# Recurrent-memory attention with a routed MLP: which queue loads the left sums, and where the routed rows are read back

## The chip, the cores and the metric

The kernel runs on one core of a Trainium2 chip. The metric is the device time of one execution in microseconds; lower is better. Engines are TensorE (PE, with its weight loads as PEld), VectorE (DVE), ScalarE (ACT), GpSimd (POOL) and SyncE (SP). SyncE, ScalarE and GpSimd can issue transfers (DMAs); SyncE's and ScalarE's go out on hardware queues, GpSimd's on a software queue, and all of them run on the core's 16 DMA engines.

## The reference

For one sequence of 2048 tokens of width 1024 the output is the sum of the input, an attention with a memory that is handed from segment to segment, and an MLP that only two tokens take.

```
x  = A_x                                   # 2048 x 1024
xn = layernorm(x)
# attention: 64 segments of 32 tokens, 32 heads of 128
for s in range(64):
    h = concat([mem, xn[32 s : 32 s + 32]])          # 8 + 32 rows
    q, k, v = h Wq, h Wk, h Wv
    o = softmax(mask(q k^T / sqrt(128))) v Wo
    mem = o[:8];  A[32 s : 32 s + 32] = o[8:]
# MLP on the two tokens with the largest r = xn @ w_r
y = (silu(xs @ w_gate) * (xs @ w_up)) @ w_down       # 1024 -> 3584 -> 1024
B = xn;  B[idx] += sigmoid(r[idx]) * y
out = x + A + B
```

## The kernel before, in words

The memory makes the 64 segments a chain: a segment can begin only when the first rows of the segment before are finished. Of each segment only 24 token rows and the 8 memory rows go through the chain. The last 8 token rows of every segment (the "left" rows, 512 in all) feed nothing later. Their queries, keys and values are made once ahead of the chain; within the chain only their attention sums are made (tile OTL), and GpSimd stores them to DRAM (`ol_d`, four tensors of 16 segments each; `store_sums`, line 639). Their projection with Wo is left for the tail.

Weights of the attention are 64 granules of 512 KB. Most stay resident on the chip; the streamed ones are fetched again in every segment by SyncE, five slots ahead (`fetch`, line 401). The end of a segment is a loop over the 16 granules of Wo (`for w in range(16)`): granule w of Wo is used and, if streamed, the next fetch goes out. In the last segment, at w == 2, the space of eight resident granules (area big0) has become free. It turns into OTA, which will hold all 512 left rows' sums, 16 pieces of 256 KB (k = 0 to 15, `load_left_out`, line 629), four for each block of 128 left rows.

The order of all instructions is written out by hand; nothing is reordered. A transfer of SyncE or ScalarE, and one of GpSimd likewise, takes one of eight completion counters in turn, and waits for the transfer that had it before. So at most eight of a queue are under way.

The tail, after the last segment's Wo loop:

- SyncE's queue holds, in this order: 16 tiles of w_gate (448 KB each, issued from line 451 as homes come free during the last segment), the left sums k 4 to 7, the four blocks of x rows (XLS, line 893), six tiles of w_up, the left sums k 8 to 15, four tiles of w_up into the first half of OTA, six more w_up and 16 transfers of w_down (line 460).
- `left_sums` (line 898): VectorE takes mean and variance of the four XLS blocks and turns each into x plus its normed value.
- `left_rows_out(0)`, half A (line 919): TensorE multiplies blocks 0 and 1 of OTA with all of Wo, 64 matmuls a block into two PSUM accumulators each (tags kept0 to kept3, one buffer each). VectorE adds the accumulators to XLS (line 931), GpSimd stores the block (line 932).
- The two routed token rows are copied into a zero-padded tile RX (32 columns for each of 8 chunks, lines 949 to 951). The first 20 pieces of gate and up follow (`gate_up(0, early)`, line 959); each piece frees a home, into which SyncE fetches the next tile.
- An activation of one column asks for the Silu table (line 969). Then half B, `left_rows_out(1)`: blocks 2 and 3, into the same four accumulators.
- GpSimd reads the two routed rows of the output back from DRAM into ROW (line 973). Their place is only known at run time, so the read-back stands behind every store of the output. The other 12 pieces of up follow, Silu of gate on ScalarE (line 982), the product (line 985), transposes, and w_down (line 1001, YP, 112 matmuls).
- VectorE adds YP times the gate value to ROW (line 1004); SyncE stores the first row, ScalarE the second (line 1006). The program then closes with a drain of each engine and a barrier (line 1037).

Of the kernel before, what the change touches and what calls it, by code (L numbers as in the profile page):

```python
# [12 lines left out]
ACTF = mybir.ActivationFunctionType  # L13
# [17 lines left out]
def kernel(  # L31
# [16 lines left out]
    nc = tc.nc  # L48
    P = 128
    Bsz, S, D = A_x.shape  # L50
# [8 lines left out]
    KC = D // P  # L59
# [70 lines left out]
    def room(g, name):  # L130
        if g not in place:
            return home(g, [P, 2048], BF16, name)[:, :]
        tag, i = place[g]
        return areas[tag][:, i, :]
# [23 lines left out]
    I8 = CT[0:1, 24:32].bitcast(U32)  # L158
# [34 lines left out]
    for s in range(4):  # L193
        nc.vector.tensor_copy(out=SELM[:, s, 0:XM, :],
                              in_=IDENT[:, 32 * s:32 * s + XM].unsqueeze(2).to_broadcast([P, XM, 4]))
# [104 lines left out]
    RXT = const.tile([P, 2 * KC], BF16, name="RXT").rearrange("p (k c) -> p k c", c=2)  # L300
    SIG = const.tile([P, 1], F32, name="SIG")
    routed_rows = []
# [134 lines left out]
    moe = [("gu", w, kc, fh) for w in range(2) for kc in range(KC) for fh in range(2)]  # L437
# [191 lines left out]
    def load_left_out(k, queue):  # L629
        queue.dma_start(out=areas["big0"][:, 4 * k:4 * k + 4, :], in_=ol_d[k // 4][:, 4 * (k % 4):4 * (k % 4) + 4, :])  # L630
# [39 lines left out]
    for s in range(NSEG):  # L670
# [178 lines left out]
        for w in range(16):  # L849
            if w == 5:  # L850
                attend(1, 0)
            if w == 8:
                attend(1, 1)
            if w == 2 and s + 1 == NSEG:
                OTA = area("big0", [P, NSEG, XL * H], "OTA")
                for k in range(4):
                    load_left_out(k, nc.gpsimd)
            Gv = granule(48 + w)
            if s + 1 == NSEG and 48 + w in streamed:
                left_in_slots[48 + w] = Gv  # L860
            project(WO, w, Gv, lhs_main, w == 15)
            if w == 9 and s + 1 < NSEG:
                load_qkl(s + 1)
                bring_back(FIRST_KEPT, 1, "bE", nc.scalar.copy)
                bring_back(FIRST_KEPT, 2, "kt", nc.vector.tensor_copy)
            if w == 11 and s + 1 == NSEG:
                store_sums()
            if w == 10 and s + 1 < NSEG:
                nxt["st"] = new_st(s + 1)
            after(s, 48 + w)  # L870
# [9 lines left out]
            ST = nxt["st"]  # L880


    for k in range(4, 8):
        load_left_out(k, nc.sync)
    WOS = {g: res_tiles.get(g, left_in_slots.get(g)) for g in sorted(range(48, 64), key=lambda g: g in streamed)}
    XLS = [room(resident[k], "XLS") for k in range(2)]
    T2 = one.tile([P, 512], BF16, tag="bC", name="T2")
# [10 lines left out]
    def left_sums():  # L898
        ml = T2[:, 100:108].rearrange("p (t c) -> p t c", c=2)
        sl = T2[:, 108:124].bitcast(F32).rearrange("p (t c) -> p t c", c=2)  # L900
        for t in range(4):
            row_stats(left_x(t), T2[:, 128:152].bitcast(F32).rearrange("p (c s) -> p c s", c=2), ml[:, t, :])
        sd_rows(ml, T2[:, 124:128])
        nc.vector.tensor_copy(out=sl[:, :, 0], in_=ml[:, :, 0])
        nc.vector.reciprocal(out=sl[:, :, 1], in_=ml[:, :, 1])
        for t in range(4):
            m, r = sl[:, t, 0:1], sl[:, t, 1:2]
            nc.vector.tensor_scalar(out=m, in0=m, scalar1=r, scalar2=-1.0, op0=ALU.mult, op1=ALU.mult)
            nc.vector.tensor_scalar(out=r, in0=r, scalar1=1.0, scalar2=None, op0=ALU.add)
            nc.vector.tensor_scalar(out=left_x(t), in0=left_x(t), scalar1=r, scalar2=m, op0=ALU.mult, op1=ALU.add)  # L910
# [8 lines left out]
    def left_rows_out(k):  # L919
        WD = [[psK.tile([P, 512], F32, name=f"WD{2 * b + c}", tag=f"kept{2 * b + c}") for c in range(2)] for b in range(2)]  # L920
        for b in range(2):
            for i, (g, Gv) in enumerate(WOS.items()):
                for hs in range(2):
                    for c in range(2):
                        nc.tensor.matmul(WD[b][c][:, :], lhsT=OTR[:, P * (2 * k + b):P * (2 * k + b + 1), 2 * (g - 48) + hs],
                                         rhs=Gv[:, D * hs + 512 * c:D * hs + 512 * (c + 1)],
                                         start=(i + hs == 0), stop=(i == 15 and hs == 1))
            x = left_x(2 * k + b)
            for c in range(2):
                xc = x[:, 512 * c:512 * (c + 1)]  # L930
                nc.vector.tensor_tensor(out=xc, in0=xc, in1=WD[b][c][:, :], op=ALU.add)
            nc.gpsimd.dma_start(  # L932
                out=out2.rearrange("(t s r) d -> t s r d", t=4, s=16)[2 * k + b, :, XM:SEG, :], in_=x)

    T0 = room(resident[2], "T0")
    left_sums()
    left_rows_out(0)
    T3 = one.tile([P, 256], BF16, tag="bA", name="T3")
    ROW = T3[:, 0:256]

    def quarters(c):
        return T3[c:c + 97:32, 0:256]

    def routed_out(v):
        return out2[bass.ds(v, 1), :].rearrange("o (g d) -> (o g) d", g=4)

    ends = (nc.sync, nc.scalar)
    GU = [[psA.tile([P, 512], F32, tag="acc", name=f"GA{fh}") for fh in range(2)], [BS, BT]]
    RX = T2[:, 256:512].rearrange("p (k r) -> p k r", r=32)
    nc.vector.memset(T2[:, 256:512], 0.0)  # L950
    nc.vector.tensor_copy(out=RX[:, :, 0:2], in_=RXT)

    pieces = [(w, kc, fh) for w in range(2) for kc in range(KC) for fh in range(2)]

    def gate_up(i0, i1):
        for w, kc, fh in pieces[i0:i1]:
            Gt = moe_tiles["gu", w, kc, fh]
            for g in range(4):
                nc.tensor.matmul(GU[w][fh][32 * g:32 * g + 32, 0:FQ], lhsT=RX[:, kc, :], rhs=Gt[:, FQ * g:FQ * (g + 1)],
                                 start=(kc == 0), stop=(kc == KC - 1), tile_position=(0, 32 * g), skip_group_check=True)  # L960
            free_homes.append(moe_home["gu", w, kc, fh])
            fetch_moe()
# [3 lines left out]
    fetch_moe()  # L966
    early = len(moe)
    gate_up(0, early)
    nc.scalar.activation(out=T2[:, 126:127], in_=T2[:, 124:125], func=ACTF.Silu)
    left_rows_out(1)  # L970
    nc.vector.memset(ROW, 0.0)
    for c in range(2):
        nc.gpsimd.dma_start(out=quarters(c), in_=routed_out(routed_rows[c]))
    gate_up(early, len(pieces))
    assert not moe
    end_rows = [ends[c].value_load(I8[0:1, c:c + 1], min_val=0, max_val=S - 1) for c in range(2)]
    HR = T0[:, 0:2 * FQ]
    SG = [[T0[:, 1024 + 448 * i:1024 + 448 * (i + 1)].bitcast(F32) for i in range(2)],
          [one.tile([P, 224], F32, tag=tag, name="SG") for tag in ("kt", "bE")]]
    for fh in range(2):  # L980
        for i in range(2):
            nc.scalar.activation(out=SG[fh][i], in_=GU[0][fh][:, 224 * i:224 * (i + 1)], func=ACTF.Silu)
    for fh in range(2):
        for i in range(2):
            nc.vector.tensor_tensor(out=HR[:, FQ * fh + 224 * i:FQ * fh + 224 * (i + 1)], in0=SG[fh][i],
                                    in1=GU[1][fh][:, 224 * i:224 * (i + 1)], op=ALU.mult)
# [55 lines left out]
```

## Time and profile before

| | |
|---|---|
| median of 3 runs | 1846.6 us (1841.18 to 1846.63) |
| the profiled execution's own time | 1831.82 us |
| its span, first to last instruction | 1830.1 us |
| mean granted TensorE clock | 0.987 |
| busy: PE, PEld, DVE, ACT, POOL | 1551.3, 830.0, 880.2, 779.7, 325.0 us |
| HBM read, written | 652.90 MB, 29.89 MB (373 GB/s over the span) |
| SyncE's queue, GpSimd's queue | 624.84 MB, 47.59 MB |

Rows of the profile give a start in microseconds from the start of the span, the time, the engine, the line of the kernel, the operation and its tiles (output, arrow, inputs), then how many. In square brackets stands the idle time of the engine ahead of the instruction and what ended it. "SPq" and "ACTq" are the sequencers that issue transfers. A row on transfers gives the size of one and the median time from issue to landing. The matmul records of a few instructions can be missing.

### The profile page before, as it was taken

The numbers are of one execution on the slowest core, as the hardware profiler recorded it, in microseconds if no ns is written. First come the engines' busy times: TensorE is split into PE (matmuls) and PEld (weight loads), VectorE is DVE, ScalarE is ACT, GpSimd is POOL, SyncE is SP. The second block draws the span as 40 slices with busy tenths as digits, with TensorE's granted clock in tenths as the row PEclk, the third lists the DMA queues.
The fourth block names the chain that finished last, engine by engine and source line by source line (L and its number), as shares of the span: only waits on it lengthen the run. The fifth ranks groups of instructions, "written<-read, shape, count | busy, mean of one in ns | idle before, by whom it ended". The sixth has DMA issues, their size and how long they took to land. (4 is left out here: it accounts for less than half of the span.)

```text
span 1830.1 us, 70088 instructions
## 1 busy us (share of the span) xinstructions
PE 1551.3 (85%) x30198; PEld 830.0 (45%) x30210; DVE 880.2 (48%) x2716; ACT 779.7 (43%) x2028; POOL 325.0 (18%) x600
## 2 busy tenths in 40 slices
PE   8999888878888888888888888888888888888887
PEld 5444344444444444444444444444444444444445
DVE  7722155544455555555544455555554454555421
ACT  3342144444444444444444444444444444444400
POOL 1111311111111111111111111111111111111100
PEclk9999899999999999999999999999999999999989
DMA  9876999999999999999999999999999999999996
GB/s 357 303 278 189 304 373 394 375 365 382 372 393 396 394 397 389 396 394 396 391 380 387 395 386 397 394 395 395 388 384 378 360 398 390 391 399 391 392 364 226
DMA packets 216423, 678.48 MB, mean 371 GB/s; under 512 B 42800, under 2 KB 46176, under 8 KB 216112
## 3 DMA queue, kind: packets, MB, share of 16 engines
q1 hardware_dynamic: 190664, 624.84, 89.3%
q0 software_dynamic: 24576, 47.59, 7.6%
q8 instruction: 236, 3.87, 0.9%
q10 hardware_dynamic: 872, 1.58, 0.2%
q14 instruction: 75, 0.61, 0.1%
HBM read 652.90 MB, written 29.89 MB: 373 GB/s over the span
## 5 line engine op out<-in xcount | busy, mean ns | idle before, releaser
L795 PE MATMUL PSm<-wres,ST 128*32 128x512 bf16 x6400 | 501.1, 383 | 0.0
L795 PEld LDWEIGHTS <-ST 128*32 128x32 bf16 x12288 | 314.5, 96 | 343.2 <-issue 100.9
L795 PE MATMUL PSm<-g,ST 128*32 128x512 bf16 x3080 | 306.5, 384 | 44.6 <-DMA g<-wsc 40.6
L424 ACT COPY BK<-KEPT 128x512 bf16<-128x512 bf16 x315 | 189.3, 601 | 175.8 <-PE WO L842 64.6
L842 PEld LDWEIGHTS <-OT 128*32 128x32 bf16 x8192 | 209.0, 97 | 83.4 <-issue 67.7
L804 ACT CAST XB<-PSm 128x512 bf16<-128x512 f32 x256 | 150.3, 587 | 121.4 <-PE PSm L795 119.8
L691 DVE COPY KT<-BT 128x512 bf16<-128x512 bf16 x126 | 51.0, 405 | 288.4 <-PE BT L681 288.4
L842 PE MATMUL WO<-W8B,OT 128*32 128x256 bf16 x4096 | 188.7, 278 | 0.6 <-issue 0.4
L795 PE MATMUL PSm<-W8A,ST 128*32 128x512 bf16 x2048 | 182.8, 380 | 0.0
L622 POOL DMA_DIRECT2D QKL<-ql_d x63 | 46.8, 742 | 745.7 <-ACT OTL L763 729.5
L842 PE MATMUL WO<-g,OT 128*32 128x256 bf16 x2560 | 131.2, 277 | 49.2 <-DMA g<-wsc 44.1
L876 POOL DMA_DIRECT2D out_dram<-XN x256 | 130.5, 525 | 172.9 <-DVE XN L872 167.0
L823 ACT CAST VM<-PSm 128x512 bf16<-128x512 f32 x128 | 80.1, 626 | 115.0 <-PE PSm L795 114.9
L424 DVE COPY BK<-KEPT 128x512 bf16<-128x512 bf16 x189 | 80.3, 425 | 72.2 <-ACT BK L424 36.8
L681 PEld LDWEIGHTS <-XB 128*128 128x128 bf16 x1024 | 58.1, 98 | 105.9 <-ACT XB L804 99.2
L723 DVE TENSOR_REDUCE DN<-BS 128x8 f32<-128x320 f32 x128 | 62.9, 492 | 86.4 <-ACT BS L718 86.4
L681 PE MATMUL BT<-IDENT,XB 128*128 128x128 bf16 x1024 | 101.9, 222 | 2.3
L686 ACT COPY QT<-BT 128x512 bf16<-128x512 bf16 x128 | 75.0, 586 | 59.9 <-PE BT L681 57.6
L708 DVE TENSOR_TENSOR BS<-BS,CT 128x96 f32<-128x96 f32 (+1 forms) x256 | 59.7, 233 | 83.2 <-PE BS L701 78.7
L795 PE MATMUL PSm<-BK,ST 128*32 128x512 bf16 x567 | 76.5, 388 | 22.2 <-DVE ST L387 22.2
L522 PE MATMUL PSG<-XLT,wres 128*128 128x512 bf16 x336 | 93.1, 379 | 0.8 <-ACT GA L524 0.7
L348 POOL DMA_DIRECT2D XN<-in_A_x_dram x64 | 34.9, 546 | 311.4 <-PE PSm L795 149.8
(196 smaller groups left out, 2291.4 us busy)
## 6 DMA issues: line engine op xcount, KB each, us to landing
g<-wsc SPq DMA_DIRECT2D x1071, 512.0 KB, 6.3
ql_d<-GA POOLq DMA_DIRECT2D x16, 512.0 KB, 6.7
QKL<-ql_d POOLq DMA_DIRECT2D x63, 128.0 KB, 6.2
MW<-in_B_w_gate_dram SPq DMA_DIRECT2D x16, 448.0 KB, 9.1
wres<-in_A_Wk_dram SPq DMA_DIRECT2D x12, 512.0 KB, 10.2
MW<-in_B_w_down_dram SPq DMA_DIRECT2D x12, 512.0 KB, 11.4
MW<-in_B_w_up_dram SPq DMA_DIRECT2D x12, 448.0 KB, 8.3
XP<-in_A_x_dram SPq DMA_DIRECT2D x8, 512.0 KB, 9.3
```

What stands on the lines that cost most here:

```text
L424: copy(out=back[g][c], in_=KEPT_COLS[g][c])
L522: nc.tensor.matmul(PSG[:, :], lhsT=part(Gs[kc], h // 4)[:, P * (h % 4):P * (h % 4 + 1)], rhs=XLT[:, :, kc, :], start=(kc == 0), stop=(kc = ...
L681: nc.tensor.transpose(out=PTq[:, il, :, :].rearrange("p j r -> p (j r)"), in_=XB[:, il * P:(il + 1) * P], identity=IDENT[:, :])
L686: nc.scalar.copy(out=QT[half][:, :, :], in_=pv)
L691: (nc.vector.tensor_copy if s else nc.scalar.copy)(out=KT[half][:, :, 0:32], in_=pv)
L708: nc.vector.tensor_tensor(out=S4, in0=S4, in1=m, op=ALU.add)
L723: nc.vector.tensor_reduce(out=DN[:, :], in_=S8, axis=AX.X, op=ALU.add)
L795: nc.tensor.matmul(PSm[32 * jq:32 * jq + 32, :], lhsT=ST[:, kc, :], rhs=part(Gv, jq), start=(kc == 0), stop=(kc == KC - 1), tile_position= ...
L804: nc.scalar.copy(out=XB[:, :], in_=PSm[:, :])
L823: nc.scalar.copy(out=VM[half][:, :], in_=PSm[:, :])
L842: nc.tensor.matmul(PS[32 * g:32 * g + 32, 0:256], lhsT=lhs(h), rhs=Gv[:, D * hs + 256 * g:D * hs + 256 * (g + 1)], start=False, stop=(last ...
L876: nc.gpsimd.dma_start(out=out2[s * SEG:s * SEG + XM, 256 * g:256 * (g + 1)], in_=OB[32 * g:32 * g + XM, :])
```

## The change

Four things change, all in the tail.

1. The left sums k 4 to 7 are loaded by GpSimd, at w == 2 of the last segment and behind k 0 to 3; SyncE's loads of them go.
2. The padded tile RX is made ahead of `left_sums`, and no longer behind half A.
3. Silu of gate stands right behind the first 20 pieces of gate and up, in front of half B; the activation of one column goes.
4. The fourth store of left rows is issued by ScalarE, and no longer by GpSimd. The two routed rows are read back by SyncE and ScalarE, each with the row number that it also uses for its final store; GpSimd reads nothing back.

```diff
             if w == 2 and s + 1 == NSEG:
                 OTA = area("big0", [P, NSEG, XL * H], "OTA")
-                for k in range(4):
+                for k in range(8):
                     load_left_out(k, nc.gpsimd)
...
-    for k in range(4, 8):
-        load_left_out(k, nc.sync)
     WOS = {g: res_tiles.get(g, left_in_slots.get(g)) for g in sorted(range(48, 64), key=lambda g: g in streamed)}
...
-            nc.gpsimd.dma_start(
+            (nc.scalar if k and b else nc.gpsimd).dma_start(
                 out=out2.rearrange("(t s r) d -> t s r d", t=4, s=16)[2 * k + b, :, XM:SEG, :], in_=x)
...
     T0 = room(resident[2], "T0")
+    RX = T2[:, 256:512].rearrange("p (k r) -> p k r", r=32)
+    nc.vector.memset(T2[:, 256:512], 0.0)
+    nc.vector.tensor_copy(out=RX[:, :, 0:2], in_=RXT)
     left_sums()
     left_rows_out(0)
...
-    RX = T2[:, 256:512].rearrange("p (k r) -> p k r", r=32)
-    nc.vector.memset(T2[:, 256:512], 0.0)
-    nc.vector.tensor_copy(out=RX[:, :, 0:2], in_=RXT)
...
     early = len(moe)
     gate_up(0, early)
-    nc.scalar.activation(out=T2[:, 126:127], in_=T2[:, 124:125], func=ACTF.Silu)
-    left_rows_out(1)
-    nc.vector.memset(ROW, 0.0)
-    for c in range(2):
-        nc.gpsimd.dma_start(out=quarters(c), in_=routed_out(routed_rows[c]))
-    gate_up(early, len(pieces))
-    assert not moe
-    end_rows = [ends[c].value_load(I8[0:1, c:c + 1], min_val=0, max_val=S - 1) for c in range(2)]
+    assert early >= 2 * KC
     HR = T0[:, 0:2 * FQ]
...
             nc.scalar.activation(out=SG[fh][i], in_=GU[0][fh][:, 224 * i:224 * (i + 1)], func=ACTF.Silu)
+    left_rows_out(1)
+    nc.vector.memset(ROW, 0.0)
+    end_rows = [ends[c].value_load(I8[0:1, c:c + 1], min_val=0, max_val=S - 1) for c in range(2)]
+    for c in range(2):
+        ends[c].dma_start(out=quarters(c), in_=routed_out(end_rows[c]))
+    gate_up(early, len(pieces))
+    assert not moe
```

On GpSimd, from w == 2 of the last segment to the end of the program, there stood (T_40198 is ROW; OTL the last segment's left sums; "ISA" a register instruction):

```order
L630 DMA OTA<-ol_d_101 128x1024 x4
L639 DMA ol_d_104<-OTL 128x256
L876 DMA out_dram<-XN 24x256 x4
L932 DMA out_dram<-XLS 16x8x1024 x4
L973 ISA
L973 DMA T_40198<-out_dram 4x256
L973 ISA
L973 DMA T_40198<-out_dram 4x256
L1037 UNCONDITIONAL_BRANCH
```

and there stands now:

```order
L630 DMA OTA<-ol_d_101 128x1024 x4
L630 DMA OTA<-ol_d_102 128x1024 x4
L639 DMA ol_d_104<-OTL 128x256
L876 DMA out_dram<-XN 24x256 x4
L930 DMA out_dram<-XLS 16x8x1024 x3
L1035 UNCONDITIONAL_BRANCH
```

Four loads have come in ahead of the last segment's stores; one store of left rows and both read-backs have gone from its end.

On SyncE, from the gate tiles on (ol_d_102 holds k 4 to 7, ol_d_103 and ol_d_104 hold k 8 to 15), there stood:

```order
L451 DMA MW<-in_B_w_gate_dram 128x1792 x16
L630 DMA OTA<-ol_d_102 128x1024 x4
L893 DMA XLS<-in_A_x_dram 128x1x1024 x4
L451 DMA MW<-in_B_w_up_dram 128x1792 x6
L630 DMA OTA<-ol_d_103 128x1024 x4
L630 DMA OTA<-ol_d_104 128x1024 x4
```

and there stands now:

```order
L451 DMA MW<-in_B_w_gate_dram 128x1792 x16
L891 DMA XLS<-in_A_x_dram 128x1x1024 x4
L451 DMA MW<-in_B_w_up_dram 128x1792 x6
L630 DMA OTA<-ol_d_103 128x1024 x4
L630 DMA OTA<-ol_d_104 128x1024 x4
```

The four loads are gone from between gate and XLS; the rest keeps its order, down to the last w_down tile. Behind that tile SyncE now reads its row number, reads its row back and stores it.

On ScalarE, behind the square root of the left rows' statistics (L259), there stood (T_40031 and SG are the Silu of gate, GA the gate accumulators):

```order
L969 ACT_TABLE_LOAD
L969 ACTIVATE T_40006<-T_40006 128x1
L976 TENSOR_LOAD CT
L976 ISA x2
L982 ACTIVATE T_40031<-GA_40199 128x224 x2
L982 ACTIVATE SG<-GA_40200 128x224 x2
L1006 ISA
L1006 DMA out_dram<-T_40198 4x256
```

and there stands now:

```order
L973 ACT_TABLE_LOAD
L973 ACTIVATE T_40031<-GA_40201 128x224 x2
L973 ACTIVATE SG<-GA_40202 128x224 x2
L930 DMA out_dram<-XLS 16x8x1024
L976 TENSOR_LOAD CT
L976 ISA x2
L978 ISA
L978 DMA T_40200<-out_dram 4x256
L1004 ISA
L1004 DMA out_dram<-T_40200 4x256
```

The one-column activation is gone with the table load left in its place; a store of left rows and a read-back stand ahead of the final store.

## The prediction

> **What bounds the kernel now.** I read the page first, then the rows of the program's closing line (L1037), the timeline of the last fifteen microseconds, TensorE's timeline of the tail, stretches of the tail with DMA rates, SyncE's queue waits, and single transfers. The page says how long the span is and that the DMA engines are busy in nearly every slice:
>
> ```profile
> span 1830.1 us, 70088 instructions
> ...
> DMA  9876999999999999999999999999999999999996
> ```
>
> So a transfer that is moved to another queue still takes its time on the same engines. All that the change touches runs after about 1728 us. The end comes first; these are the closing instructions, with durations min/median/max in ns and the starts of the first and the last:
>
> ```profile
> L1037 POOLq EVENT_SEMAPHORE  x4: 17/17/17, 1829.3 to 1830.0; - x4
> L1037 POOLq DRAIN  x3: 46/115/10832, 1818.5 to 1829.8; - x3
> L1037 SPq DRAIN  x3: 7/7/7, 1826.0 to 1829.5; - x3
> L1037 PEldq DRAIN  x2: 13/464/915, 1819.2 to 1829.6; - x2
> L1037 DVEq DRAIN  x2: 19/258/497, 1821.5 to 1829.6; - x2
> L1037 ACTq DRAIN  x2: 8/82/157, 1825.1 to 1829.5; - x2
> ```
>
> Each engine drains and then reports to a barrier. SyncE reports at 1826.0, ScalarE at 1825.3, TensorE and VectorE before that. GpSimd drains for 10.83 us from 1818.5, until 1829.3, and only then goes on to the barrier: 3.3 us behind SyncE. The remaining 0.8 us to 1830.1 is the barrier. Before that stands this:
>
> ```profile
> 1816.84 3.23 PE L1001 MATMUL YP<-MW,T 128*2 128x256 bf16 x112
> 1817.84 1.24 POOL L973 DMA_DIRECT2D T<-out_dram  x2 [3.87 <-DMA out_dram<-XLS]
> 1821.45 0.48 DVE L1004 SCALAR_TENSOR_TENSOR T<-YP,SIG,T 128x256 bf16<-128x256 f32 x1 [4.67 <-DMA T<-out_dram]
> 1821.96 0.71 SPq L1006 DMA_DIRECT2D out_dram<-T  x1
> 1823.94 1.16 ACTq L1006 DMA_DIRECT2D out_dram<-T  x1
> ```
>
> TensorE is done at 1820.07. The last addition starts at 1821.45, because GpSimd's read-back of the two routed rows has only just landed, and ends at 1821.93. From there to SyncE's report are 4.1 us: two stores one behind the other. TensorE's own path through the tail:
>
> ```profile
> 1751.40 4.48 PE L925 MATMUL WD<-g,OTA 128*128 128x512 bf16 x19
> 1762.50 9.38 PE L925 MATMUL WD<-W8B,OTA 128*128 128x512 bf16 x32 [6.61 <-DMA OTA<-ol_d]
> ...
> 1774.30 4.48 PE L925 MATMUL WD<-g,OTA 128*128 128x512 bf16 x20
> 1780.29 3.21 PE L959 MATMUL GA<-MW,T 128*32 128x448 bf16 x64 [1.51 <-DVE T L951]
> ...
> 1784.47 6.85 PE L925 MATMUL WD<-W8B,OTA 128*128 128x512 bf16 x31 [0.21 <-issue]
> ...
> 1798.06 7.07 PE L925 MATMUL WD<-W8B,OTA 128*128 128x512 bf16 x32
> ...
> 1807.56 4.48 PE L925 MATMUL WD<-g,OTA 128*128 128x512 bf16 x20
> ```
>
> It waits 6.61 us for the left sums of half A's second block and 1.51 us for the padded rows. The third stall is hidden in a duration: the 32 matmuls after the long wait take 9.38 us, where the same 32 take 7.07 at 1798.06. The stretches (PE, PEld, DVE, ACT, POOL busy, granted clock, DMA share, GB/s) show a clock of 0.65 there:
>
> ```profile
> 1731.00:1755.00 24.00, 20.61 (x215) 13.27 (x213) 2.22 (x7) 1.86 (x8) 2.56 (x5) 0.86 1.02 398
> 1758.00:1766.00 8.00, 3.50 (x9) 1.46 (x10) 2.60 (x5) 0.00 (x0) 0.00 (x0) 0.65 1.06 276
> 1774.00:1784.00 10.00, 8.49 (x103) 4.91 (x101) 4.01 (x10) 0.64 (x3) 1.11 (x2) 1.00 0.94 331
> 1784.00:1798.00 14.00, 13.74 (x70) 9.21 (x65) 0.00 (x0) 0.47 (x2) 0.00 (x0) 1.00 1.04 397
> 1798.00:1806.00 8.00, 8.00 (x38) 5.29 (x37) 1.29 (x2) 0.00 (x0) 0.53 (x1) 1.00 1.08 218
> ```
>
> Two kinds of low rate must be told apart: at 276 and 218 GB/s the engines are busy (share above 1), so each packet is slow; at 331 the share is 0.94, so they had nothing to do. The reason for the latter, and the transfer that ends the weights:
>
> ```profile
> SPq L451 <- PE WD L925: 3.9, 1, 3.9
> SPq L451 <- PE GA L959: 3.2, 6, 1.2
> 1806.44 0.37 SPq L460 DMA_DIRECT2D MW<-in_B_w_down_dram  x1
> MW<-in_B_w_down_dram SPq DMA_DIRECT2D x1, 512.0 KB, 10.0
> ```
>
> SyncE's queue stood still behind half A and behind gate. The last w_down tile landed at 1816.4, 0.4 us before its consumer began. So transfers are the second bound, right behind TensorE.
>
> **The change part by part.** *Left sums k 4 to 7 on GpSimd.* They go out right behind k 0 to 3, ahead of all gate weights, where SyncE sent them behind these. The 6.61 us wait goes, and with it the slow clock: 9.38 - 7.07 = 2.31 us. What they cost is 1 MB beside the last streamed weights of segment 63. The rows of before: GpSimd's issues, a weight tile issued just ahead of them, and the last one, issued amid them:
>
> ```profile
> 1728.42 2.15 POOL L630 DMA_DIRECT2D OTA<-ol_d  x4 [11.41 <-PE PSm L795]
> g<-wsc SPq DMA_DIRECT2D x1, 512.0 KB, 6.1
> g<-wsc SPq DMA_DIRECT2D x1, 512.0 KB, 8.9
> ```
>
> Issuing four more takes GpSimd 2.15 us; behind them waits only its store of the last left sums, which half B reads. The first MB cost the last weight tile 2.8 us. The second costs between 0 (it arrives behind that tile) and 1.05 MB at 398 GB/s = 2.6 us; I take 1.5, since it joins late. The Trainium skill, "DMA: Bandwidth & Descriptors", section on queues, rings and completion order, says that a DMA engine goes round-robin between the queues that have work, packet by packet; by that rule the four cannot hide behind SyncE's transfers but take their share at once, which agrees with 8.9 against 6.1.
>
> SyncE's later transfers do not come sooner: the bytes ahead of them are the same. So the XLS rows land as before, and this decides what is late next:
>
> ```profile
> 1763.33 1.29 DVE L254 BATCH_NORM_STATS2 T<-XLS 128x6 f32<-128x512 bf16 x2 [22.24 <-DMA XLS<-in_A_x_dram]
> ...
> 1775.20 1.28 DVE L931 TENSOR_TENSOR XLS<-XLS,WD 128x512 bf16<-128x512 bf16 x2
> ```
>
> VectorE frees the first two accumulators at 1776.5. TensorE will have ended half A at 1778.78 - 8.92 = 1769.9 and gate at 1774.1 (1784.47 - 1780.29 = 4.2 later), and half B needs those accumulators: it waits 2.4 us. The delay of 1.5 above lies inside that wait.
>
> *Padded rows ahead of half A.* Two small VectorE operations move into its 22.24 us of idle time; TensorE's 1.51 us goes. *Silu right behind gate.* ScalarE had waited 10.47 us for gate and has nothing else to do there:
>
> ```profile
> 1783.36 0.61 ACT L982 ACTIVATE T<-GA 128x224 f32<-128x224 f32 x2 [10.47 <-PE GA L959]
> ```
>
> The warming activation goes, but the table load still stands ahead of that wait, and the product with up comes a whole half later. Nothing.
>
> *TensorE's path* to the end of YP, if every weight is there: 1820.07 - 6.61 - 2.31 - 1.51 + 2.4 = 1812.0.
>
> *Transfers.* SyncE no longer waits for half A or gate; of the 10 us at 331 GB/s, 10 x (1 - 331/397) = 1.7 us come back. The fourth store of left rows (256 KB, 0.7 us) now falls inside the stream, where before it came behind it. Last landing 1816.4 - 1.7 + 0.7 = 1815.4. Its 8 of the 112 matmuls take 0.23 us at full clock, twice that at half; with that TensorE ends at 1815.8. Transfers then bind, 3.8 us above TensorE's own path.
>
> *Fourth store on ScalarE, read-back on SyncE and ScalarE.* The rows of before for two such stores, the third (in the 218 GB/s stretch) and the fourth (alone), and for one read-back in the chain:
>
> ```profile
> out_dram<-XLS POOLq DMA_DIRECT2D x1, 256.0 KB, 8.2
> out_dram<-XLS POOLq DMA_DIRECT2D x1, 256.0 KB, 3.6
> 1818.48 2.77 DMA T<-out_dram
> ```
>
> Half B ends at 1803.9 (before: 1812.0, and TensorE's 8.1 us behind it stay). VectorE adds 1.29: 1805.2. The store runs amid w_down: 3.6 to 8.2 us; I take 8.2 x 218/397 = 4.5, landing at 1809.7. The read-back takes 2.8 more on ScalarE's empty queue: 1812.5. SyncE's stands behind the last w_down tiles: up to 1815.4 and a little. I take 1815.6, still under TensorE's 1815.8. If that cover were gone, each microsecond of it would count in full.
>
> *The end.* The addition starts at 1815.9 and ends at 1816.4; plus 4.1 and 0.8 is a span of 1821.3. GpSimd now has its last work at about 1791.6 (third store); even 10.83 us of drain end near 1803. The Trainium skill, "VectorE: DVE Perf Modes", section "The DRAIN you can't avoid", has the DRAINs of the pre- and postamble at a constant 12 ns or so on all five engines; the 10,832 ns row differs, and the row decides. By the page nothing would be won here.
>
> **Sum.** 1830.1 - 1821.3 = 8.8 us: 5.5 up to the last addition, 3.3 from the drain. The profiled execution's own time is 1831.8 us, so 1823.0 by its own measure. It ran 14.8 us under the median of the runs shown, 1846.6; the differences are taken over, since nothing in the tail scales with that: 1837.8.
>
> **The rivals.**
> *TensorE binds (0.15).* The two busy stretches at 276 and 218 GB/s lost 8 x (1 - 276/397) = 2.4 and 3.6 us, and nothing shows that they belong to these transfers. Without them the weights are in at 1809.4, XLS lands 2.4 earlier and half B's wait goes: TensorE ends at 1809.6, but the read-back at 1801.5 + 1.3 + 4.5 + 2.8 = 1810.1 is now last. The addition ends at 1810.7, the span at 1815.6: gain 14.5, less what before would also shed. 1832.1.
> *The read-back takes the place of the wait (0.13).* If the fourth store lands only with the last weights, 1815.4 + 1.0, the read-back (2.8 and its issue) ends 3.0 later, the addition at 1820.0, the span at 1824.9: gain 5.2, 1841.4. For it: the one store of before amid w_down needed 8.2 us, and SyncE's read-back stands behind w_down in its own queue. Against: 8.2 us from 1805.2 is 1813.4, still ahead of the weights.
> *The drain stays last (0.10).* If GpSimd's 10.83 us is a closing cost that ends 3.3 us behind SyncE whatever it issued, the change does not do that part: gain 5.5, 1841.1. Against: it starts right behind its last issue.
> *Slower (0.05).* The second MB holds up the last streamed weight. Beyond 2.4 us each microsecond lengthens TensorE's path, from 6.2 (2.4 + 3.8) it binds, and to lose the 8.8 it must reach 15.0; past 0.3% (5.5 us) 20.5, which gives 1852.1. At 398 GB/s its whole MB is 2.6, so it would take a queue that stalls, as no row of before shows.
>
> **How the numbers follow.** The forecast has the rest, 0.57, and alone runs from 1835.5 to 1840.5 (1.5 us of landing either way, 2 us of read-back, the state of the chip). The range reaches to the first two rivals, 1832.0 to 1842.5, and leaves out about 0.15. 0.3%, about what a measurement of this kernel can tell from no change, is 5.5 us. Faster by more: nearly all of the forecast, the first rival and a little of the drain's, less what runs between 1841.18 and 1846.63 blur: 0.75. Within: 0.19. Slower: 0.06.
>
> **What would show it.** Right: no wait of TensorE for OTA, the 32 matmuls near 7 us, a new wait of some 2 us of half B on VectorE, no SyncE wait for WD, YP stretched out and waiting for w_down, ScalarE's store of 4 to 5 us, GpSimd's drain over by 1805, a barrier right behind SyncE. Wrong: an end still set by GpSimd's drain; YP's 112 matmuls in one piece; the last addition waiting over 1 us for the read-back; a last weight granule over 12 us from issue to landing.

## The result, and the profile after

| | before | changed kernel |
|---|---|---|
| median | 1841.15 us (20 runs, 1829.52 to 1849.35) | 1828.74 us (20 runs, 1820.04 to 1848.23) |
| ratio | | 0.9936, 95% interval 0.9915 to 0.9957 |
| the profiled execution's own time, span | 1831.82, 1830.1 us | 1832.24, 1830.6 us |
| addition of the routed rows | 1821.45 us | 1825.26 us |
| from its start to the end of the span | 8.65 us | 5.34 us |
| the tail (below) | 101.7 us | 94.0 us |

The change is faster by 0.64%, 11.8 us of 1841.15 (7.9 to 15.6 by the interval). I had forecast 8.8 us and 1837.8 us, with a range down to 1832.0; the measured time lies 3.3 us under that range.

The two profiled executions ran equally long, although one kernel is faster. The difference hides in the body: GpSimd issues its first load of left sums 1728.42 us into the span before, and 1736.62 us after, 8.2 us later, ahead of everything that the change touches. So from here on the **tail** is read: from that issue to the end of the span. A "+" is a time in the tail.

The changed kernel's page, first its span and its DMA slices:

```profile
span 1830.6 us, 70101 instructions
DMA  9886899999999999999999999999999999999998
```

Its closing instructions (durations min/median/max in ns, first and last start):

```profile
L1035 POOLq DRAIN  x3: 46/115/11689, 1803.1 to 1830.3; - x3
L1035 SPq DRAIN  x3: 7/7/7, 1829.7 to 1830.0; - x3
L1035 ACTq DRAIN  x2: 8/250/492, 1828.3 to 1830.1; - x2
```

GpSimd's long drain now begins at 1803.1 and is over at 1814.8. SyncE reports last, at 1829.7, 0.9 us before the end. The timeline of the last fifteen microseconds:

```profile
1815.37 1.29 DVE L929 TENSOR_TENSOR XLS<-XLS,WD 128x512 bf16<-128x512 bf16 x2 [12.53 <-PE WD L923]
1816.69 0.64 ACTq L930 DMA_DIRECT2D out_dram<-XLS  x1
1820.35 3.38 PE L999 MATMUL YP<-MW,T 128*2 128x256 bf16 x112
1822.95 0.67 SPq L978 DMA_DIRECT2D T<-out_dram  x1
1823.05 1.38 ACTq L978 DMA_DIRECT2D T<-out_dram  x1
1825.26 0.48 DVE L1002 SCALAR_TENSOR_TENSOR T<-YP,SIG,T 128x256 bf16<-128x256 f32 x1 [4.97 <-DMA T<-out_dram]
1825.77 0.63 SPq L1004 DMA_DIRECT2D out_dram<-T  x1
1827.68 0.62 ACTq L1004 DMA_DIRECT2D out_dram<-T  x1
```

YP runs in one piece and ends at 1823.73; the addition starts 1.5 us behind it, because the routed rows land only then. TensorE's timeline from the last streamed weights to half B:

```profile
1748.76 7.47 PE L923 MATMUL WD<-W8B,OTA 128*128 128x512 bf16 x32
...
1762.97 7.07 PE L923 MATMUL WD<-W8B,OTA 128*128 128x512 bf16 x32
...
1776.88 3.21 PE L957 MATMUL GA<-MW,T 128*32 128x448 bf16 x64
...
1784.96 9.87 PE L923 MATMUL WD<-W8B,OTA 128*128 128x512 bf16 x32 [4.11 <-DVE XLS L929]
```

The waits for OTA (6.61) and for the padded rows (1.51) are gone, and the 32 matmuls of half A's second block take 7.07 us instead of 9.38. The new wait in front of half B is 4.11 us, and the 32 matmuls behind it take 9.87 us where the same 32 take 7.07. VectorE's rows say what it waits for:

```profile
1772.36 1.28 DVE L254 BATCH_NORM_STATS2 T<-XLS 128x6 f32<-128x512 bf16 x2 [22.71 <-DMA XLS<-in_A_x_dram]
...
1784.22 2.47 DVE L929 TENSOR_TENSOR XLS<-XLS,WD 128x512 bf16<-128x512 bf16 x4
```

The statistics start when the first XLS block has landed, at +35.7, and the addition that frees an accumulator comes 11.9 us later. From there the chain of waits of the changed kernel goes (start, time):

```profile
1785.56 29.79 PE WD L923 x126
1815.37 1.29 DVE XLS L929 x2
1816.69 6.11 DMA out_dram<-XLS
...
1823.05 2.08 DMA T<-out_dram
```

So in this execution the end is set by half B, the fourth store and the read-back. The read-back lands at 1825.1. The weights stand level with TensorE's own path: the last w_down tile landed at 1823.3, 0.4 us before YP's end. Three stretches of the tail (columns as before):

```profile
1767.00:1774.00 7.00, 7.00 (x35) 4.61 (x34) 1.57 (x4) 0.00 (x0) 0.00 (x0) 1.00 1.05 258
1785.00:1795.00 10.00, 9.98 (x34) 5.05 (x34) 1.69 (x3) 0.00 (x0) 1.11 (x2) 0.73 1.00 365
1808.00:1815.00 7.00, 7.00 (x34) 4.63 (x33) 0.00 (x0) 0.00 (x0) 0.00 (x0) 1.00 1.05 277
```

The clock of 0.73 is the price of half B's wait. The two stretches with busy DMA engines and a low rate are still there, at 258 and 277 GB/s. SyncE's queue no longer waits for half A (3.9 us before) or for gate (3.2). Behind the streamed weights its transfers wait for TensorE only once, behind half B and ahead of the last w_down tile:

```profile
SPq L460 <- PE WD L923: 0.3, 1, 0.3
```

One profile below, that of the new end alone, is from a slower execution than the others, but the clock granted in its tail, 0.92, is no lower than in before's tail, 0.91.

### The profile page after: what moved, and what is told of

Its sections match the earlier page's. It is cut to its first block, busy times and chain, and to the rows that moved or that the text cites. A ratio compares the mean times of both kernels' runs of the same rounds, so it can differ in the third digit from the quotient of the medians.

```text
span 1830.6 us, 70101 instructions
## 1 busy us (share of the span) xinstructions
PE 1553.9 (85%) x30210; PEld 828.1 (45%) x30210; DVE 880.2 (48%) x2716; ACT 779.7 (43%) x2027; POOL 325.0 (18%) x601
## 5 line engine op out<-in xcount | busy, mean ns | idle before, releaser
L842 PEld LDWEIGHTS <-OT 128*32 128x32 bf16 x8192 | 206.3, 97 | 92.9 <-issue 78.0
L708 DVE TENSOR_TENSOR BS<-BS,CT 128x96 f32<-128x96 f32 (+1 forms) x256 | 59.7, 233 | 82.5 <-PE BS L701 78.0
L522 PE MATMUL PSG<-XLT,wres 128*128 128x512 bf16 x336 | 93.1, 379 | 0.9 <-ACT GA L524 0.7
L872 DVE CAST XN<-WO 128x256 bf16<-128x256 f32 x64 | 27.2, 425 | 131.7 <-PE WO L842 131.7
```

The source lines that it names most:

```text
L522: nc.tensor.matmul(PSG[:, :], lhsT=part(Gs[kc], h // 4)[:, P * (h % 4):P * (h % 4 + 1)], rhs=XLT[:, :, kc, :], start=(kc == 0), stop=(kc = ...
L708: nc.vector.tensor_tensor(out=S4, in0=S4, in1=m, op=ALU.add)
L842: nc.tensor.matmul(PS[32 * g:32 * g + 32, 0:256], lhsT=lhs(h), rhs=Gv[:, D * hs + 256 * g:D * hs + 256 * (g + 1)], start=False, stop=(last ...
```

## The experiments

The tails first, to read the rest by. Ratios are of the runs' times to those of before on the same chip; 0.3% is 5.5 us.

| run | tail, us | ratio (95%) |
|---|---|---|
| before; once more | 101.7; 102.0 | |
| changed kernel; once more | 94.0; 90.4 | 0.9936 (0.9915 to 0.9957) |
| before + new end (items 3, 4) | 98.3 | 0.9966 (0.9935 to 0.9997) |
| before + loads (item 1) | 101.5 | 1.0004 (0.9964 to 1.0044) |
| before + padding (item 2) | 97.8 | 1.0018 (0.9988 to 1.0048) |
| change without its new end | 99.3 | 0.9972 (0.9937 to 1.0007) |
| change + XLS first | 92.3 | 0.9947 (0.9916 to 0.9978) |
| change + XLS on GpSimd | 90.1 | 0.9964 (0.9937 to 0.9991) |
| XLS and half B's sums first | 91.8 | 0.9944 (0.9904 to 0.9983) |
| and w_down's halves on two queues | 89.8 | 0.9947 (0.9920 to 0.9973) |
| and the fourth store in two | 90.9 | 0.9948 (0.9917 to 0.9978) |
| and XLS on GpSimd | 91.4 | 0.9980 (0.9950 to 1.0010) |

**The two kernels once more**, without an edit, each one profile.

> The kernel before once more, without an edit, to see how far its tail repeats from one execution to another: 101.7 us within 1.0 if the tail's lengths can be compared from single profiles; if it differs by 3 or more, the gains of the experiments under 3 us are not to be told from noise by one profile.

> The changed kernel once more, without an edit: its tail is 94.0 us within 1.0 if single profiles can be compared, and half B's wait for VectorE comes again (about 4 us, with a slow clock behind it); if that wait is under 2.5, as I forecast at first, the forecast was not wrong there and the one profile was.

Before's tail repeats in its length, 102.0 us, less so in its parts: half A waits 8.36 us for OTA there (6.61), and 7.7 us lie between the last addition and the end (8.65). The changed kernel's doesn't repeat: 90.4 us, 3.6 shorter. TensorE's timeline and the end of that second execution, then two rows of its chain of waits:

```profile
1742.84 9.56 PE L923 MATMUL WD<-W8B,OTA 128*128 128x512 bf16 x32
...
1777.61 0.38 PE L923 MATMUL WD<-W8B,OTA 128*128 128x512 bf16 x1 [0.59 <-DVE XLS L929]
1778.21 6.85 PE L923 MATMUL WD<-W8B,OTA 128*128 128x512 bf16 x31 [0.22 <-DVE XLS L929]
...
1815.22 0.39 PE L999 MATMUL YP<-MW,T 128*2 128x256 bf16 x8 [0.89 <-DMA MW<-in_B_w_down_dram]
1815.93 0.48 DVE L1002 SCALAR_TENSOR_TENSOR T<-YP,SIG,T 128x256 bf16<-128x256 f32 x1 [5.40 <-DMA T<-out_dram]
```

```profile
1806.92 6.56 DMA out_dram<-XLS
...
1813.73 2.06 DMA T<-out_dram
```

Here half A starts on a slow clock (9.56 for 7.47), so TensorE ends gate later and VectorE sooner (its statistics start at +34.2): half B waits 0.8 us in two pieces and its clock stays up. YP now waits for w_down, as in my forecast, and ends at 1815.61. But the store and the read-back are still last: the read-back lands at 1815.79, 0.2 us behind YP, and the addition follows. So the read-back ends the chain in both executions, by 1.5 us and by 0.2; how near the other paths come changes from one execution to the next, and one profile places an end to about 4 us, not to 1. What follows from gains under 3 us below is read from rows that the edit touches, not from the sum.

**The new end alone** (before with the Silu, the fourth store and the read-back moved):

```diff
-            nc.gpsimd.dma_start(
+            (nc.scalar if k and b else nc.gpsimd).dma_start(
...
-    for c in range(2):
-        nc.gpsimd.dma_start(out=quarters(c), in_=routed_out(routed_rows[c]))
+    for c in range(2):
+        ends[c].dma_start(out=quarters(c), in_=routed_out(end_rows[c]))
```

> The kernel before with items 3 and 4 of the change alone: Silu right behind gate, the fourth store on ScalarE, the read-backs on SyncE and ScalarE; the left sums k 4 to 7 stay on SyncE and the padded rows behind half A. Measured is the tail, from GpSimd's first load of left sums at w == 2 to the end of the span: 1830.1 - 1728.4 = 101.7 us before, 1830.6 - 1736.6 = 94.0 with the whole change. My theory (the 7.7 us come from two separate places, TensorE's waits and the end of the program): TensorE keeps its waits of 6.6 and 1.5 us; GpSimd's drain is over long before the end (3.3 us), and the read-back lands before TensorE's end instead of 1.2 us behind it; tail 97.1, so 4.6 us shorter. Rival A (all of it is the end of the program, and what TensorE gains is given back at the XLS rows): tail 94. Rival B (the end of the program gives nothing): 101.7.

The end of its timeline and its closing rows:

```profile
1838.77 3.23 PE L1001 MATMUL YP<-MW,T 128*2 128x256 bf16 x112
1842.05 0.48 DVE L1004 SCALAR_TENSOR_TENSOR T<-YP,SIG,T 128x256 bf16<-128x256 f32 x1 [3.33 <-PE YP L1001]
```

```profile
L1037 POOLq DRAIN  x3: 46/115/13112, 1821.5 to 1846.9; - x3
L1037 SPq DRAIN  x3: 7/7/7, 1846.3 to 1846.6; - x3
```

The drain is over at 1834.6, far ahead of SyncE at 1846.3; the addition follows YP at once; the waits of 6.34 and 1.51 us stay. The tail is 98.3 us, 3.4 under before, where I expected 4.6. From the addition to the end it is 5.1 us, 3.5 less than before, so the drain's part came in full; YP ended at +93.1, and at +91.6 before, so the read-back's part does not show. The new end works by itself, and the ratio agrees (0.9966).

**The loads alone** (before with the four loads on GpSimd).

```diff
-                for k in range(4):
+                for k in range(8):
                     load_left_out(k, nc.gpsimd)
...
-    for k in range(4, 8):
-        load_left_out(k, nc.sync)
```

> The kernel before with item 1 alone: left sums k 4 to 7 on GpSimd. My theory, from the trace of the change: half A ends some 9 us sooner, but the padded rows stand behind VectorE's additions, and these behind the statistics of the XLS rows, which land as late as before (35 us into the tail). So gate begins at about 50.5 us into the tail against 51.9 before, with a cold clock behind 10 us of idle time, and that gives the 1.4 us back: tail 101.7, within 1.5. By the prediction's addition of separate terms (6.61 and 2.31 off, 2.4 back) it would be 6.5 us shorter, 95.2. Either way the end of the program stays GpSimd's drain.

TensorE's gate in its timeline:

```profile
1791.23 5.71 PE L957 MATMUL GA<-MW,T 128*32 128x448 bf16 x64 [6.85 <-DVE T L949]
```

The wait for OTA is gone, and a wait for the padded rows of 6.85 us stands in its place, with gate at 5.71 us for 3.21 behind it. Those rows are written by VectorE behind half A's additions, and these wait for XLS. Tail 101.5, ratio 1.0004: alone, the loads give nothing. My prediction had priced this wait at its old 1.51 us and taken it away as a term of its own; in truth the padding ahead of half A is what lets the loads pay.

**The padding alone** (before with the three lines on RX moved ahead of `left_sums()`).

> The kernel before with one part of the change alone: the padded rows are made ahead of half A instead of between the halves; the loads and the end stay as before. By the prediction's separate terms this part removes the 1.51 us wait of TensorE between the halves and its slow clock behind it, nothing else: TensorE is 1.5 us earlier and the tail (from GpSimd's first load of left sums for half A to the end of the span) is about 100.2 us for 101.7 before, if the read-back at the end follows in full. The rival, that the parts only work together: alone this part gives 0 to 0.5 (tail 101.2 to 101.7), because what ends the tail is then the end of the transfers and GpSimd's closing drain; with the loads alone having given 0.2, the two alone sum to less than the 2.4 that loads and padding gave together with the end undone.

TensorE's waits in its timeline:

```profile
1776.76 8.93 PE L925 MATMUL WD<-W8B,OTA 128*128 128x512 bf16 x32 [6.78 <-DMA OTA<-ol_d]
...
1792.53 3.21 PE L959 MATMUL GA<-MW,T 128*32 128x448 bf16 x64
```

The padded rows' wait went and the one for OTA stayed, as expected. But the tail came out at 97.8, below both expectations, while 12 timed runs show no gain (1.0018; a gain of 1.5 us would be 0.9992, inside the interval). Of the 3.9 us, 1.5 are the wait that went. Another 1.6 are the left sums, which landed that much sooner than in before; the edit moves no transfer, so I take these as luck. That the loads give nothing without the padding is read from the wait in the run before, not from sums: by tails, the two parts alone gave 0.2 and 3.9 us, more than the 2.4 of the next run, which has both; by times, they show no gain (1.0004 and 1.0018) where the next run shows 0.9972, and the intervals overlap.

**The change without its new end** (the fourth store and the read-backs on GpSimd again).

```diff
-            (nc.scalar if k and b else nc.gpsimd).dma_start(
+            nc.gpsimd.dma_start(
...
-        ends[c].dma_start(out=quarters(c), in_=routed_out(end_rows[c]))
+        nc.gpsimd.dma_start(out=quarters(c), in_=routed_out(routed_rows[c]))
```

> The whole change with item 4 undone: fourth store and both read-backs on GpSimd again. My theory: TensorE runs as in the changed kernel (half B behind a wait for VectorE of 4 us, YP ending some 87 us into the tail), the last addition stays where it is, since GpSimd's store and read-back took 9.3 us behind half B before and 9.8 in the changed kernel, but GpSimd's drain is last again, 3.3 us behind the others: tail 97.3. Rival A (all of the gain is the end of the program): 101.7. Rival B (the end of the program gives nothing): 94.0.

Half B in its timeline, then its closing rows:

```profile
1790.37 0.38 PE L923 MATMUL WD<-W8B,OTA 128*128 128x512 bf16 x1 [2.29 <-DVE XLS L929]
1790.96 8.54 PE L923 MATMUL WD<-W8B,OTA 128*128 128x512 bf16 x31 [0.22 <-DVE XLS L929]
```

```profile
L1035 POOLq DRAIN  x3: 46/115/11158, 1828.9 to 1840.6; - x3
L1035 SPq DRAIN  x3: 7/7/7, 1835.1 to 1840.4; - x3
```

GpSimd drains until 1840.1 and SyncE has long reported, at 1835.1: the drain is last again, now by 5.0 us. Tail 99.3, 2.0 more than expected, 1.7 of it because the drain ends 5.0 us behind the rest and not 3.3. Up to half B this is the changed kernel, so it is a third look at that wait: 2.29 and 0.22 us, and a slow clock (8.92 for 7.07).

**XLS first** (the change, with the four XLS loads issued by SyncE at w == 0 of the last segment, ahead of all gate tiles), to see what half B's wait is worth.

```diff
+            if w == 0 and s + 1 == NSEG:
+                load_xls(nc.sync)
...
-    for t in range(4):
-        nc.sync.dma_start(out=left_x(t), in_=x_left[t, :, XM:SEG, :])
```

> The whole change, and the four XLS loads moved on SyncE's queue ahead of all gate tiles (issued at w == 0 of the last segment). My theory (behind TensorE's wait stand the transfers, at nearly the same height): VectorE has its statistics long before half A ends, half B begins right behind gate, 4.1 us of waiting and 2.8 us of slow clock go; but the last w_down tile lands as before, 86.7 us into the tail, YP now waits for it, and the tail shortens by 1 to 1.5 us, to 92.8. Rival (TensorE's own path alone sets the end): 6.9 us shorter, 87.1. On the 8 us at about 250 GB/s that lie 30 us into the tail: if they come from the XLS loads, whose rows go out in groups of eight, they move with them to the first 15 us of the tail; if from the place in the program, they stay.

```profile
1793.73 8.78 PE L929 MATMUL WD<-W8B,OTA 128*128 128x512 bf16 x32 [3.31 <-DMA OTA<-ol_d]
```

This row of its timeline shows the wait for VectorE turned into one of 3.31 us for half B's own left sums. The slow stretch moved with the loads: 302 GB/s from 10 to 17 us into the tail, and 406 from 30 to 35, where the changed kernel has 255. Tail 92.3, as expected within 0.5, but not for the reason I gave. The end of its timeline:

```profile
1828.03 3.23 PE L1005 MATMUL YP<-MW,T 128*2 128x256 bf16 x112
1832.69 0.48 DVE L1008 SCALAR_TENSOR_TENSOR T<-YP,SIG,T 128x256 bf16<-128x256 f32 x1 [4.72 <-DMA T<-out_dram]
```

YP does not wait for w_down, whose last tile landed at +84.9 and not as late as before. The read-back is last again, behind a store of 5.9 us, and the addition starts 1.4 us behind YP.

**XLS on GpSimd**, behind the eight loads (`load_xls(nc.gpsimd)` at w == 2, otherwise as above).

> The whole change, and the XLS loads issued by GpSimd behind its eight loads of left sums. In the run with XLS first on SyncE the slow stretch (about 260 GB/s for 8 us) had moved from 30 to 37 us into the tail to 10 to 18, with the XLS loads. If it comes from how SyncE's queue spreads these row groups over the engines, GpSimd's transfer of the same rows does not bring it: about 400 GB/s there, the last w_down tile 2.4 us sooner than with XLS first on SyncE (about 82.5 us into the tail), half B's wait for its left sums down from 3.3 to about 1 us, tail about 90. If it comes from the rows themselves, it stays, and the tail is that of XLS first on SyncE, 92.3.

Half B waited 1.86 us for its left sums, its 32 matmuls took 7.10, and the tail was 90.1, the expected value. The reason I gave for it did not hold: the slow stretch came along to GpSimd's queue (292 GB/s from 15 to 20 us into the tail, where I expected 400), and the last w_down tile landed at +84.5, not +82.5. The match is luck.

**XLS and half B's sums first** (XLS first, and left sums k 8 to 11 ahead of the six w_up tiles).

```diff
+    for k in range(8, 12):
+        load_left_out(k, nc.sync)
     fetch_moe()
-    for k in range(8, 16):
+    for k in range(12, 16):
         load_left_out(k, nc.sync)
```

> XLS first on SyncE, and the left sums k 8 to 11 ahead of the six w_up tiles. With XLS first TensorE waited 3.3 us for them ahead of half B and ran 1.7 us slow behind that. My theory (transfers and TensorE stand at nearly the same height at the end): this wait goes, half B begins right behind gate, YP could begin 5 us sooner, but the last w_down tile lands as before, 85 us into the tail; the read-back comes off the end, so that the last addition follows YP directly: tail 91.0, 1.3 us shorter. Rival (TensorE alone binds): 5 us shorter, 87.3.

No wait is left in front of half B. Its stretches near the end, and the first of YP's late pieces:

```profile
1803.00:1810.00 7.00, 7.00 (x35) 4.63 (x33) 0.00 (x0) 0.00 (x0) 0.00 (x0) 1.00 1.06 310
1810.00:1817.00 7.00, 7.00 (x84) 4.56 (x82) 2.92 (x9) 0.00 (x0) 0.00 (x0) 1.00 1.04 306
```

```profile
1820.63 0.39 PE L1007 MATMUL YP<-MW,T 128*2 128x256 bf16 x8 [0.76 <-DMA MW<-in_B_w_down_dram]
```

TensorE gained and waits for w_down instead; the last tile landed at +85.8. Tail 91.8 (expected 91.0; the rival's 87.3 is out). Once TensorE's waits are gone the transfers bind.

**w_down's halves on two queues** (the run before; four of the w_down transfers, two pairs, fill 64 partitions each, and one of each pair goes to ScalarE, the other to GpSimd).

```diff
-                        nc.sync.dma_start(out=t3[x0 - P * j:x1 - P * j, :, :],
+                        q = nc.sync if x1 - x0 == P else (nc.scalar, nc.gpsimd)[f]
+                        q.dma_start(out=t3[x0 - P * j:x1 - P * j, :, :],
```

> As the kernel with left sums k 8 to 11 first, and the four half tiles of w_down (64 partitions each) taken off SyncE's queue: the lower halves on ScalarE's, the upper ones on GpSimd's. My theory: the second slow stretch (220 to 270 GB/s, 66 to 73 us into the tail) belongs to these half tiles, which write to half of the partitions one after the other; on two queues at once they write to all, the stretch goes, w_down is in 3 us sooner (82 us into the tail) and the tail is about 88.5. Rival (the stretch belongs to w_down, or to the place): it stays where it was, tail 91.

Three stretches of it, the first with the halves under way:

```profile
1780.00:1787.00 7.00, 7.00 (x39) 4.50 (x32) 0.00 (x0) 2.39 (x5) 0.58 (x1) 1.00 1.05 316
1787.00:1794.00 7.00, 7.00 (x35) 4.61 (x33) 0.00 (x0) 0.00 (x0) 0.00 (x0) 1.00 1.00 348
...
1808.00:1815.00 7.00, 6.94 (x149) 4.95 (x152) 3.14 (x9) 0.00 (x0) 0.00 (x0) 1.00 1.05 390
```

The late slow stretch is gone, but a milder one has come where the two queues issued the halves (1779 to 1781): by 397 GB/s, 14 us at 310 and 306 lost 3.1 us, and 14 us at 316 and 348 lose 2.3. Tail 89.8, between expectation and rival.

**The fourth store in two** (the run before; the last block of left rows is made and stored in two halves of 512 columns, so that the first store goes out earlier).

> As the kernel with the half tiles on two queues, and the last block of left rows made in two halves of 512 columns, one after the other, each added and stored on ScalarE's queue as it is ready, so that only 128 KB are left to store behind half B. My theory (in the changed kernel the last addition waited 1.5 us for the read-back, which stood behind a store of 6.1 us): the second store takes 3 to 5 us, the read-back is off the end; where transfers bind it gives up to 1.5 us, tail 87 to 88.5. Rival (a store's time is all latency): no change.

Tail 90.9; the addition stands directly behind YP, as it did without the edit, and YP waits for w_down, landed at +84.9. The second store, of half the bytes, was no quicker: the read-back went out 6.6 us behind its issue, as in the run before, where I expected 3 to 5 us. The rival, no change, holds. But the store was not late in this version; the split was not tried on the changed kernel itself, where it is.

**XLS on GpSimd as well** (the version with w_down's halves on two queues; `load_xls` moves from SyncE at w == 0 to GpSimd at w == 2).

> The change with the left sums of half B first among the late loads, the four 64-partition pieces of w_down spread over ScalarE and GpSimd, and the row-group loads of half B's left sums on GpSimd behind the eight loads instead of on SyncE. Theory: both slow stretches of the transfers are then gone, the last of w_down lands at +81.3 us and the tail is about 87.4 (94.0 with the change, 89.8 with the last load order and the row groups on SyncE). Rival: GpSimd's issues become the bound, the row groups land late there and half B waits for them on VectorE by over 2 us: tail 90 or more.

Its two slow stretches:

```profile
1751.00:1763.00 12.00, 12.00 (x58) 7.80 (x55) 4.17 (x10) 0.00 (x0) 3.14 (x6) 0.96 1.04 319
...
1787.00:1799.00 12.00, 12.00 (x57) 8.06 (x56) 0.00 (x0) 0.93 (x4) 0.00 (x0) 1.00 1.04 313
```

Both theories fell. The slow stretches came along to the other queues, the last w_down tile landed at +85.5 and the tail was 91.4. The rival's tail (90 or more) came out without its reason, since half B did not wait for VectorE. None of these versions has a lower ratio than the change's own 0.9936.

## Why the prediction was right and wrong

**The level failed, not the gain.** The step of the prediction that failed is "the differences are taken over ... 1837.8": I hung 8.8 us on the median of three runs, 1846.6, though the profiled execution stood at 1831.8. Twenty runs put the median of before at 1841.15; the same 8.8 gives 1832.4, and the measured 11.8 gives 1829.4. On the old level the measured gain would have given 1834.8, inside my range. In the sets beside the experiments before's medians were 1838.0, 1836.3 and 1834.3 us (35, 27 and 23 runs), so the level differs by some microseconds even between larger sets. The spread was there to see: 14.8 us between one execution and the median of three others is more than the gain. A range around a median of three has to hold that median's own error, here 5.5 us; mine, with 5.8 us below and 4.7 above, had room for the cases alone. The spread comes from the body: among the profiles of this study the tail began between 1721.6 and 1745.8 us (that of the new end alone left out), and a repeat of before moved by 6.8 us there and by 0.3 in its tail.

**The drain: right.** 3.3 us were forecast. From the addition's start to the end of the span it was 8.65 us before and 7.74 in its repeat, 5.34 after and 5.37 in the repeat, so 2.4 to 3.3 us went; undoing the new end brings the drain back as the last thing. The rival of a drain that stays last is out. The drain itself was not shortened (10.83 us before, 11.69 after): it was moved ahead of the end. The Trainium skill's constant 12 ns or so ("VectorE: DVE Perf Modes", section "The DRAIN you can't avoid") does not hold for this drain.

**TensorE's three losses: right in sum, wrong as separate terms.** 6.61, 2.31 and 1.51 us all went, and the loads cost nothing that shows: half A begins at +12.1 and +12.0, and at +12.4 in the repeat of before. But the loads alone only moved the wait to the padded rows (6.85 us), so item 1 pays only together with item 2. Both made, the wait moves once more, behind gate, where 20 pieces of work lie ahead of it.

**Half B's new wait: right in place and in mean, its clock left out.** I forecast 2.4 us. Three executions that are alike up to there show 4.11, 0.81 and 2.51, mean 2.5: it is the difference of two paths, TensorE's end of gate (+44.2 to +46.5) and VectorE's first free accumulator (+46.7 to +48.8). Missing is the slow clock behind it, 2.8 us after 4.11, 1.85 after 2.51 and 0.2 after 0.81, though before's own 9.38 row had shown such a price.

**The transfers: mis-sized.** I put the last landing 1.0 us earlier (+87.0 by before's tail). It was +86.7, then +84.3, for +88.0 and +87.8 before. The DMA engines' total from the tail's start to that landing, before, after and in the repeat:

```profile
DMA packets 12216, 30.89 MB, mean 351 GB/s; under 512 B 1328, under 2 KB 1376, under 8 KB 12209
```

```profile
DMA packets 12007, 30.84 MB, mean 356 GB/s; under 512 B 1326, under 2 KB 1374, under 8 KB 11999
```

```profile
DMA packets 12024, 30.88 MB, mean 366 GB/s; under 512 B 1331, under 2 KB 1383, under 8 KB 12016
```

The bytes are the same and the rate differs, even between two executions of one kernel; why it does stays open. "Transfers then bind, 3.8 us above TensorE" was wrong in the first execution, where the two are level, and too large elsewhere: YP waited 1.5 us for w_down in the repeat, not at all with XLS first, and 1.3 to 3.2 us in the five versions after that one.

**The fourth store: too cheap, and so its cover failed.** I took 4.5 us, scaling 8.2 by the transfer rate. On ScalarE, amid w_down, it took 6.1, 6.6 in the repeat and 5.9 with XLS first, and the store of half the bytes was no quicker, so scaling by the rate has no support here. The read-back was to be hidden behind YP; it was last by 1.5, 0.2 and 1.4 us in these three. That is the mechanism of the second rival, at less than its price of 3.6 us (8.8 - 5.2). Two of my signs of being wrong, YP in one piece and a wait of over 1 us for the read-back, are in the first profile and not in the repeat.

**The first rival** (TensorE binds, slow stretches gone) is out: the stretches stayed. **Slower** is out. The Silu right behind gate was not tried by itself; that it costs nothing is argued, not shown.

Put together, the tail was forecast at 101.7 - 8.8 = 92.9 us and measured at 94.0 and 90.4. The times say 11.8 (7.9 to 15.6), so the gain of 8.8 was within what was measured.

## What to carry to other kernels

Before a difference is hung on a median, ask how well that median is known: three runs that spread over 5 us, with a fourth 9 us below them, can't carry a range of 10 us. When two waits stand one behind the other on the same source (here XLS, VectorE, accumulators and padded rows), price their removal together, because removing the first alone only lengthens the second. A wait of 2.5 us or more on TensorE cost its clock here as well, so a new wait in a forecast needs that second term. A path that a forecast calls hidden needs its own margin: here the read-back had 0.2 us of it, and it was last.

## What the runs showed of the hardware

- **GpSimd's closing drain** is long in every run, 6.3 to 13.1 us, and it starts at GpSimd's last issue: 10.8 in both executions of before, 11.7 and 10.8 in those of the changed kernel. With its last transfer near the end of the program it set the end, by 3.3 us in before and by 5.0 in the change without its new end.
- **The clock behind a wait.** The 32 matmuls that take 7.07 us took 9.38 behind 6.61 us, 9.61 behind 8.36, 8.93 behind 6.78, 9.87 behind 4.11, 8.78 behind 3.31 and 8.92 behind 2.51, but 7.10 behind 1.86. The Trainium skill, "TensorE: Matmul & The Clock Gate", section "Part 1: The HAM clock gate", has the array go to half clock after an idle window of about 3.4 us that runs free of the program; the rows agree but for those behind 3.31 and 2.51 us, which are shorter than a window.
- **Slow transfers.** Two kinds of loads ran at 258 and 277 GB/s with the DMA engines busy, where the rest ran near 397: the XLS blocks, gathered as groups of 8 rows, and the w_down pieces of 64 partitions. Issued earlier, each took its slow stretch along. Moved to GpSimd's and ScalarE's queues they still made stretches of 313 to 348. Why is open.
- **A store amid loads.** The 256 KB store of left rows took 5.9 to 6.6 us on ScalarE's queue amid w_down, and one of 128 KB about as long.
